# One core, a long convolution and a gated feed-forward block, forward and backward: exponent tables and d h kept on chip, two allocation stacks, and DMA transposes inside the forward DFTs

## Chip, cores and metric

The kernel runs on one core of one Trainium2 chip. The metric is the device time of one execution in microseconds (us); lower is better. The kernel before takes 1195.09 us (median of 4 runs, 1191.68 to 1198.79). Engines are named as in the profile: PE is TensorE, PEld its weight loads, DVE is VectorE, ACT is ScalarE, POOL is GpSimd, SP is SyncE; SPq is SP's instruction stream, which issues nearly all DMAs here. Each of these engines takes its own instructions in order. "d h" is the gradient at xn @ w1, "generation" the making of the convolution kernel K, and KF the tile that takes K out of PSUM.

## The reference, cut to what matters

L = 2048 positions, D = 512 channels, N = 128 states, F = 1792 hidden units, bf16 in and out. The kernel computes the output and the gradients of eleven inputs.

```python
xn = layernorm(x)
dt = exp(log_dt)[:, None]
P  = exp((dt * A)[:, :, None] * arange(L))            # 512 x 128 x 2048, complex: never built whole
K  = einsum("dn,dnl,dn->dl", C, P, dt * B).real       # the convolution kernel, one row per channel
y  = irfft(rfft(pad(xn)) * rfft(pad(K)))[:L] + xn * Dskip
g  = silu(silu(xn @ w1) @ w2)                         # the FFN gate
out = x + y * g
# and the vjp of all this for grad_out: d x, d A, d B, d C, d log_dt, d Dskip, d w1, d w2
```

## The kernel before

The program is a list of Python generators. Each `yield` ends a piece of work, and `interleave` deals the pieces of two generators alternately into the in-order instruction streams. The stages run in this order:

```python
    half = gen_half(k)                     # exponent tables of all four blocks -> DRAM (k.hd)
    ...
    interleave([half, gf], [1, 2])         # beside the FFN forward
    run(gf)
    ...                                    # pools closed, new pools opened
        run(gen_ssm_fwd(k, 0))             # convolution kernel ("generation") of block 0, alone
        for b in range(1, NB):
            interleave([gen_ssm_fwd(k, b), gen_conv(k, b - 1)], [1, 2])   # three mixed stages
        run(gen_conv(k, NB - 1))           # the last block's convolution, alone
        ...
        run(gen_dw2(k))                                        # weight gradient of w2
        interleave([gen_ffn_bwd(k), gen_ssm_bwd(k)], [1, 2])   # d h to DRAM, d x; gradients of the states
        run(gen_dw1(k))                                        # weight gradient of w1 (d h read back transposed)
        run(gen_ssm_final(k))                                  # parameter gradients, tail
```

A forward DFT (three per block, twelve in all) works in two steps with a transpose of 1 MB between them. TensorE does the transpose, and ACT evicts it (`ev` is `nc.scalar.copy` here):

```python
    B = big.tile([P, 2, G, P], BF16, name="dftB", tag="dftB")
    for g0 in range(0, G, 8):
        for c in range(2):
            pt = psumT.tile([P, 8, P], BF16, name="pt_b", tag="pt")
            for gi in range(8):
                nc.tensor.transpose(out=pt[:, gi, :], in_=A[:, c, g0 + gi, :, :]..., identity=k.ident[:])
            ev(B[:, c, g0:g0 + 8, :], pt[:])
        yield
```

The tables are made block by block. POOL copies parts of them (the last lines of `gen_half`), and the whole goes through DRAM:

```python
        for h in range(2):
            nc.gpsimd.tensor_copy(out=vXH[:, h, 0:2, :, :, 1], in_=vXH[:, h, 0:2, :, :, 0])
            nc.gpsimd.tensor_copy(out=vYL[:, h, :, :, 1]..., in_=vYL[:, h, :, :, 0]...)
            yh = T4[:, h, OYH:HSZ].rearrange("p (a u) -> p a u", u=2)
            nc.gpsimd.tensor_copy(out=yh[:, :, 1], in_=yh[:, :, 0])
            nc.gpsimd.tensor_scalar(out=T4[:, h, OXH + 2048:OYL], in0=T4[:, h, OXH + 1024:OXH + 2048], scalar1=-1.0, ...)
        nc.sync.dma_start(k.hd[:, 2 * b:2 * b + 2, :], T4[:])
```

At the end of each piece of generation, two ACT evictions take the kernel values out of PSUM. PSUM holds them as (q, j); SBUF wants (j, q) with 64 values of q in a row:

```python
            for e in range(2):
                es = slice(64 * e, 64 * e + 64)
                k.ev_k(KF[es, :, qb:qb + QCH].rearrange("p j q -> p q j"), ps[es, :, e, :])
```

## Time and profile before

The engine totals stand first in the profile's page: busy time, its share of the span of 1186.1 us, and the number of instructions.

```profile
PE 775.2 (65%) x6033; PEld 459.1 (39%) x6033; DVE 744.3 (63%) x1126; ACT 650.0 (55%) x1091; POOL 136.7 (12%) x96
...
```

No engine is near full over the whole, so the stages have to be read one by one. This is the view of windows of the kernel before: the stretch, its length, the busy time of each engine with the count of its instructions, then the granted clock of TensorE (PEclk, as a share of full speed), the busy share of the DMA engines, and GB/s.

```profile
core 0: us, PE busy (x) PEld busy (x) DVE busy (x) ACT busy (x) POOL busy (x), PEclk, DMA share, GB/s
...
30.00:308.00 278.00, 131.29 (x512) 50.77 (x511) 210.54 (x244) 160.50 (x319) 120.03 (x46) 0.73 0.40 145
308.00:385.00 77.00, 50.53 (x627) 43.42 (x628) 57.34 (x95) 47.52 (x61) 0.00 (x0) 0.72 0.65 217
385.00:488.00 103.00, 78.17 (x983) 62.91 (x983) 78.35 (x120) 93.93 (x146) 0.00 (x0) 0.88 0.41 122
...
695.00:763.00 68.00, 48.79 (x424) 34.02 (x421) 27.83 (x37) 52.54 (x93) 0.78 (x1) 0.87 0.19 47
763.00:859.00 96.00, 56.78 (x225) 22.89 (x226) 8.56 (x9) 4.09 (x7) 6.23 (x2) 0.82 0.96 220
859.00:1109.00 250.00, 195.75 (x960) 87.54 (x958) 162.60 (x271) 81.06 (x148) 0.00 (x0) 0.88 0.82 223
...
```

| stretch, us | what runs | what the line shows |
|---|---|---|
| 30 to 308 | FFN forward and tables | 278 us, and nothing is full: PE 131, DVE 211 of 278 us; POOL 120 |
| 308 to 385 | generation of block 0 alone | DVE 57 of 77 us |
| 385 to 695 | three mixed stages of about 103 us | ACT 94 of 103 us: the fullest engine |
| 695 to 763 | last convolution alone | ACT 53 of 68 us |
| 763 to 859 | w2 gradient | DMA share 0.96, PE 57 of 96 us |
| 859 to 1186 | backward, w1 gradient, tail | PE 196 of the first 250 us |

The change touches three pieces of work here (KF, the POOL copies, and the DFT transposes with their evictions to dftB); Vb stands beside them for comparison. A group's line reads: source line, engine, operation, output and input, shapes, count, then busy us and mean ns of one, then the idle time of the engine before them and what ended most of it.

```profile
L74 ACT CAST KF<-ps_k 64x256 bf16<-64x256 f32 x64 | 84.6, 1321 | 4.1 <-PE ps_k L564 3.6
...
L74 ACT CAST Vb<-psV 128x512 bf16<-128x512 f32 x128 | 67.5, 595 | 124.5 <-PE psV L737 84.9
...
L454 POOL COPY T_370<-T_370 128x1024 bf16<-128x1024 bf16 x8 | 62.7, 7841 | 82.2 <-DVE T_370 L60 82.2
...
L74 ACT COPY dftB<-pt_b 128x1024 bf16<-128x1024 bf16 x48 | 46.2, 1054 | 3.4 <-PE pt_b L95 3.3
L95 PE MATMUL pt_b<-ident_bfloat_80,dftA 128*128 128x128 bf16 x384 | 31.8, 236 | 17.9 <-ACT dftB L74 10.7 <-ACT dftA L74 4.7 <-ACT YTf L74 2.3
...
```

Two means are odd. The kernel eviction KF takes 1321 ns for 256 values per partition, while Vb, twice as wide, takes 595 ns on the same engine. And the POOL copy takes 7841 ns on average. The view of one tile, the table T, shows that this mean hides two kinds of copy (min/median/max in ns):

```profile
L454 POOL COPY T_370<-T_370 x8: 1032/1384/26786, 82.5 to 262.5; 128x1024 bf16<-128x1024 bf16 x8
```

The waits in the FFN stage (line that waited, what ended the wait, total us, times, longest) show PE waiting for the tanh evictions 76.8 us, and DVE waiting 38.2 us until a table had gone to DRAM:

```profile
PE ps_h L478 <- ACT th L482: 76.8, 10, 35.5
DVE T_370 L60 <- DMA hd<-T_370: 38.2, 2, 22.9
...
```

### The profile page before, as it was taken

What the parts mean: (1) busy time and instruction counts of PE and PEld (TensorE: products, weight loads), DVE (VectorE), ACT (ScalarE), POOL (GpSimd) and SP (SyncE); (2) the same over time, 40 slices, a digit from 0 to 9 for tenths busy, and PEclk for the clock granted to TensorE, in tenths of its full rate; (3) what the DMA queues carried; (4) which work ended last, traced back from release to release, by engine and by line L of the source; (5) the groups of instructions that cost most, each with busy time, mean ns of one, the idle gap of its engine ahead of it and who ended that gap; (6) DMA issues with size and microseconds to landing.
All of it is one profiled execution on the core that took longest, in us unless ns stands there. A gap on an engine that the chain in (4) does not pass through costs nothing. (4 is left out here: it accounts for less than half of the span.)

```text
span 1186.1 us, 15777 instructions
## 1 busy us (share of the span) xinstructions
PE 775.2 (65%) x6033; PEld 459.1 (39%) x6033; DVE 744.3 (63%) x1126; ACT 650.0 (55%) x1091; POOL 136.7 (12%) x96
## 2 busy tenths in 40 slices
PE   1462261367477777877777777546896886867693
PEld 1220020123266656656665654412342342423242
DVE  8788665896687759857965914600076575756153
ACT  4787362745177997999799797400042332323110
POOL 3229294360000000000000000200000000000000
PEclk9896675778777988899899888778998988988697
DMA  6221506538764513841651350499876889788981
GB/s 204 59 83 46 205 21 257 212 113 306 259 212 158 178 55 120 219 151 72 159 188 54 119 123 1 114 247 203 203 240 183 236 230 245 225 221 216 204 185 47
DMA packets 273262, 194.90 MB, mean 164 GB/s; under 512 B 189666, under 2 KB 250979, under 8 KB 271651
## 3 DMA queue, kind: packets, MB, share of 16 engines
q1 hardware_dynamic: 271842, 188.13, 55.0%
q0 software_dynamic: 768, 3.67, 0.9%
q10 hardware_dynamic: 576, 2.10, 0.6%
q8 instruction: 47, 0.77, 0.3%
q14 instruction: 29, 0.23, 0.1%
HBM read 84.28 MB, written 86.25 MB: 144 GB/s over the span
## 5 line engine op out<-in xcount | busy, mean ns | idle before, releaser
L74 ACT CAST Vb<-psV 128x512 bf16<-128x512 f32 x128 | 67.5, 595 | 124.5 <-PE psV L737 84.9
L478 PE MATMUL ps_h<-XNT,W_403 128*128 128x512 bf16 x224 | 67.0, 451 | 102.9 <-ACT th L482 76.8
L519 DVE TENSOR_TENSOR X<-H 128x1024 bf16<-128x1024 bf16 x128 | 83.8, 689 | 74.5 <-PE ps_k L564 64.6
L540 PE MATMUL pf_t<-ident_bfloat_80,X 128*128 128x128 bf16 x1024 | 93.8, 254 | 49.7 <-ACT KF L74 27.3
L540 PEld LDWEIGHTS <-X 128*128 128x128 bf16 x1024 | 80.3, 116 | 60.7 <-issue 52.6
L74 ACT CAST KF<-ps_k 64x256 bf16<-64x256 f32 x64 | 84.6, 1321 | 4.1 <-PE ps_k L564 3.6
L478 PEld LDWEIGHTS <-W_403 128*128 128x128 bf16 x224 | 23.7, 109 | 160.9 <-issue 144.4
L74 ACT CAST XTf<-pf_t 128x512 bf16<-128x512 f32 x128 | 67.4, 621 | 17.3 <-PE pf_t L540 17.1
L60 DVE TENSOR_TENSOR T_370<-MG,RC 128x896 bf16<-128x896 f32 (+1 forms) x32 | 49.2, 1615 | 43.0 <-DMA hd<-T_370 38.2
L737 PE MATMUL psV<-XT,Gbd 128*128 128x256 bf16 x256 | 48.1, 323 | 40.5 <-DMA XT<-xt_d 40.2
L454 POOL COPY T_370<-T_370 128x1024 bf16<-128x1024 bf16 x8 | 62.7, 7841 | 82.2 <-DVE T_370 L60 82.2
L713 POOL MEMSET Gbd<- 64x4096 bf16 x2 | 7.0, 3505 | 493.9 <-PE ps_i_7911 L130 493.9
L495 PE MATMUL ps_o<-W_405,aT 128*128 128x512 bf16 x224 | 57.2, 415 | 5.2 <-ACT th L482 5.2
L737 PEld LDWEIGHTS <-Gbd 128*128 128x128 bf16 x256 | 34.5, 178 | 64.9 <-DMA XT<-xt_d 30.4
L662 PE MATMUL ps_da<-DOT,W2T 128*128 128x512 bf16 x224 | 57.1, 400 | 0.2
L674 PE MATMUL ps_dx<-W1T,dhT 128*128 128x512 bf16 x224 | 56.3, 408 | 0.0
L632 PEld LDWEIGHTS <-A_ft 128*128 128x128 bf16 x224 | 22.7, 105 | 73.9 <-DMA A_ft<-at_d 28.7
L74 ACT COPY dftB<-pt_b 128x1024 bf16<-128x1024 bf16 x48 | 46.2, 1054 | 3.4 <-PE pt_b L95 3.3
L564 PE MATMUL ps_k<-YY,X 128*128 128x64 bf16 x1024 | 42.7, 203 | 7.1 <-ACT KF L74 6.6
L564 PEld LDWEIGHTS <-X 128*128 128x128 bf16 x1024 | 40.7, 105 | 9.8 <-issue 8.6
L95 PE MATMUL pt_b<-ident_bfloat_80,dftA 128*128 128x128 bf16 x384 | 31.8, 236 | 17.9 <-ACT dftB L74 10.7
L74 ACT COPY YTf<-pt_t 128x1024 bf16<-128x1024 bf16 x32 | 34.6, 1080 | 13.6 <-issue 8.5
(1576 smaller groups left out, 1932.3 us busy)
## 6 DMA issues: line engine op xcount, KB each, us to landing
hd<-T_370 SPq DMA_DIRECT2D x4, 4096.0 KB, 11.9
H<-hd SPq DMA_DIRECT2D x8, 2048.0 KB, 9.1
xt_d<-XTf SPq DMA_DIRECT2D x32, 512.0 KB, 3.1
XT<-xt_d SPq DMA_DIRECT2D x32, 512.0 KB, 4.5
YT<-yt_d SPq DMA_DIRECT2D x128, 128.0 KB, 4.5
yt_d<-YTf SPq DMA_DIRECT2D x32, 256.0 KB, 2.0
ut_d<-u SPq DMA_DIRECT2D x28, 256.0 KB, 2.4
at_d<-aT SPq DMA_DIRECT2D x4, 1792.0 KB, 6.8
```

The lines of the kernel that those rows point to most:

```text
L60: nc.vector.tensor_tensor(out=out, in0=a, in1=b, op=ALU.mult)
L74: self.nc.scalar.copy(out=out, in_=in_)
L95: nc.tensor.transpose(out=pt[:, gi, :], in_=A[:, c, g0 + gi, :, :].rearrange("p t e -> p (t e)"), identity=k.ident[:])
L454: nc.gpsimd.tensor_copy(out=vYL[:, h, :, :, 1].rearrange("p c g r l -> p c g (r l)"), in_=vYL[:, h, :, :, 0].rearrange("p c g r l -> p c g ...
L478: nc.tensor.matmul(out=ps[:], lhsT=W1[:, dk, ft * P:(ft + 1) * P], rhs=XNT[:, dk, 4 * tcn:4 * tcn + 4, :], start=(dk == 0), stop=(dk == DK ...
L495: nc.tensor.matmul(out=pso[:], lhsT=aT[:, ft, tt * P:(tt + 1) * P], rhs=W2[:, ft, :], start=(ft == 0), stop=(ft == FT - 1))
L519: nc.vector.tensor_tensor(out=out.rearrange("p (r h l u) -> p r h l u", h=nh, l=4, u=2), in0=h, in1=l, op=ALU.mult)
L540: nc.tensor.matmul(out=pf[:, qi, m // 2, :], lhsT=X[:, m, q + qi], rhs=k.ident[:], start=(m % 2 == 0), stop=(m % 2 == 1))
L564: nc.tensor.matmul(out=ps[:, q].rearrange("p e j -> p (e j)"), lhsT=X[:, m, q], rhs=YY[:, m // 2, q // 2, 1, 64 * (q % 2):64 * (q % 2) + 6 ...
L662: nc.tensor.matmul(out=ps[:], lhsT=W2T[:, dk, ft * P:(ft + 1) * P], rhs=DOT[:, dk, ls], start=(dk == 0), stop=(dk == DK - 1))
L674: nc.tensor.matmul(out=ps[:], lhsT=dhT[:, ft, tt * P:(tt + 1) * P], rhs=W1T[:, ft, :], start=(ft == 0), stop=(ft == FT - 1))
L737: nc.tensor.matmul(out=psV[:, qi].rearrange("p a b -> p (a b)"), lhsT=Gbd[:, :, :, :, 32 * (q_ // 2 % 2) + 4 * c + 2 * (q_ % 2) + q_ // 4] ...
```

## The change

Its intent: (1) compute the tables in eight halves just ahead of their use, keep them in SBUF, drop the DRAM round trip and POOL's copies; (2) split SBUF into a left and a right stack of pools, so that a stage can start before the pools of the other side close. This puts seven sixteenths of the generation beside the FFN, the generation of block b+1 beside the convolution of block b, and the last convolution beside the first backward work; (3) keep d h in SBUF, so that the w1 gradient uses TensorE transposes in place of a DRAM round trip; (4) let DMA transposes do the transposes inside the forward DFTs; (5) write KF in the other order.

The diff, cut to its core (cuts marked `...`):

```diff
@@ dft_fwd
     B = big.tile([P, 2, G, P], BF16, name="dftB", tag="dftB")
-    for g0 in range(0, G, 8):
-        for c in range(2):
-            pt = psumT.tile([P, 8, P], BF16, name="pt_b", tag="pt")
-            for gi in range(8):
-                nc.tensor.transpose(out=pt[:, gi, :], in_=A[:, c, g0 + gi, :, :]..., identity=k.ident[:])
-            ev(B[:, c, g0:g0 + 8, :], pt[:])
-        yield
+    for c in range(2):
+        nc.sync.dma_start_transpose(out=B[:, c], in_=A[:, c].rearrange("p g t e -> p (g t e)"))
+    yield
@@ main
+    def pool(name, side, bufs=1):
+        return tc.tile_pool(name=name, bufs=bufs, side=side, reuse_waits="tile")
 ...
-    interleave([half, gf], [1, 2])
 ...
-        run(gen_ssm_fwd(k, 0))
-        for b in range(1, NB):
-            interleave([gen_ssm_fwd(k, b), gen_conv(k, b - 1)], [1, 2])
-        run(gen_conv(k, NB - 1))
+        interleave([gen_ffn_fwd(k), BoundedGen(gs, 42)], [1, 1])     # gs: all of the generation
 ...
+    for b in range(NB - 1):
+        upto(b)
+        interleave([BoundedGen(gs, 26), gen_conv(k, b)], [1, 2])
 ...
+    interleave([gen_conv(k, NB - 1), BoundedGen(gb, 24)], [2, 1])    # gb: backward of blocks 0 to 2
 ...
+            interleave([chain([gd, gen_dh(k)]), gb], [2, 1])         # gd: w2 gradient; gen_dh: d h and w1 gradient
+        def final():
+            yield from gen_ssm_bwd(k, NB - 1)
+            for b0, nb in ((0, NB - 1), (NB - 1, 1)):                # the final step in two parts
+                with pool("fin", "left") as k.fin:
+                    yield from gen_ssm_final(k, b0, nb)
+        with pool("dxp", "right", 2) as k.dp:
+            interleave([gen_dx(k), final()], [1, 3])
@@ gen_ssm_fwd
-                k.ev_k(KF[es, :, qb:qb + QCH].rearrange("p j q -> p q j"), ps[es, :, e, :])
+                k.ev(KF[es, :, ql:ql + QCH], ps[es, :, e, :].rearrange("p q j -> p j q"))
@@ gen_half -> ssm_prep, half_angles, half_tables: the table k.T4 stays in SBUF
-            nc.gpsimd.tensor_copy(...)           # three copies and a scaling per half
-        nc.sync.dma_start(k.hd[:, 2 * b:2 * b + 2, :], T4[:])
+        nc.vector.tensor_copy(out=bl(1), in_=bl(0))   # one small copy left, the rest by broadcast
@@ gen_dh (from gen_ffn_bwd and gen_dw1): d h stays in k.dhT
-            nc.sync.dma_start_transpose(out=DH[:, j], in_=k.dht_d[(f0 + j) * P:(f0 + j + 1) * P, :])
+                nc.tensor.transpose(out=pt[:, j, :], in_=k.dhT[:, ft, (t0 + j) * P:(t0 + j + 1) * P], identity=k.ident[:])
@@ gen_ssm_final(k, b0, nb)
-        nc.sync.dma_start(k.outs[8].rearrange("(k p) -> p k", p=P), ddt_b[:])
+        nc.sync.dma_start(k.outs[8][bs].rearrange("(k p) -> p k", p=P), ddt_b[:])
```

## The prediction

> **What bounds the kernel now.** The kernel has four stages (first and last starts of each tile's instructions): the FFN forward with the exponent tables, 30 to 305 us; the kernel-generating stage of block 0 alone, 308 to 385; four convolution blocks, three beside the next generation, about 103 us each, the last alone, 68 us, to 763; backward to 1186. No engine bounds all: busy times are PE 775, DVE 744, ACT 650 us. By windows of 40 us: in the FFN stage DVE is busiest (31 to 37 us) and waits for POOL and the table write (one line idles 38 us until the table's DMA lands); in the convolutions ACT is busy 33 to 40 of 40 us; from 760 to 840 the DMA share is 0.97 while PE has 16 and 27 of 40 us (transposed loads: two 512 KB tiles, then both weights, hold the DMA queue); afterwards PE has 25 to 40 of 40 us; the chain of waits ends in a 26 us tail.
>
> **Removed.** The tables' DRAM round trip (33 MB) and POOL's table copies (115 us on POOL). 384 PE transposes (31.8 us) with 48 evictions to dftB (ACT 46.2 us). d h written to DRAM and loaded transposed (14.7 MB). The generation of block 0 alone, the last convolution alone and the separate last gradient stage disappear as stages of their own. The eviction of the kernel (1321 ns for 64x256, 64 times) gets another order; I take it as 30% cheaper.
>
> **Added.** 24 DMA transposes, on-chip to on-chip, of 512 KB. The trace has the same size from DRAM: 14 took a median 2.3 us on the queue and 4.8 us to landing, so I estimate 7 us for the pair of one DFT, against 2.7 us PE plus 4.2 us ACT removed: about 3 us more latency per DFT, twelve times, mostly hidden except in the last block. Table work goes to DVE in eight halves, by the times of the old operations about 17 us each, and 12 us each on ACT with table switches. 280 PE transposes of d h and of the gradient, at 83 ns busy each (as the removed ones) 25 us, and 29 us of evictions. A second read of the tanh, with 45 us of DVE work moved from forward to backward.
>
> **Sum.** Engine totals hardly change; the gain is overlap. Setup to about 42 us (7 us of parameter work goes first). FFN, generation and three convolutions: DVE about 475 us, ACT about 500; at the 88% that ACT reached in the old convolutions, 560 us, to 602 (before: 695). Last convolution beside the first backward generation: 85, to 687. Second and first weight gradient and d h with two backward blocks: PE 227 us at the old 80%, 284, to 971. d x with the last block: PE 79 us, 99, to 1070, and 8 us of tail. Prediction: 1080 us, 8 in 10 between 1010 and 1165. Faster by over 2%: 0.84; within: 0.10; slower: 0.06.
>
> **What would show it.** PE without a gap like 760 to 840; no hd in the DMA list; POOL near idle; the DFT stage waiting less than 10 us for dftB's DMA; convolutions with DVE and ACT both over 85% busy.
>
> **What would make it wrong.** The on-chip transposes. The Trainium skill, "DMA: Bandwidth & Descriptors", trn3 fast-DGE section, says that on earlier generations such a transpose is pushed tile by tile; no trace here has one with an on-chip source. If it holds the queue for 10 us instead of 2, every DFT waits and blocks the other DMAs behind it: 12 times 15 us would eat the whole gain. Second: in-order engines keep DVE waiting at the table hand-over, as the table has one buffer. Third: a lower granted clock with a busier PE.

## More of the kernel before

The tail writes d log_dt, 512 bf16 values held as 128 partitions x 4, so that neighbours in DRAM come from different partitions:

```python
    with nc.allow_non_contiguous_dma(reason="1 KB"):
        nc.sync.dma_start(k.outs[8].rearrange("(k p) -> p k", p=P), ddt_b[:])
```

## The result and the profile after

The changed kernel takes 1063.2 us (median of 4 runs, 1061.63 to 1068.18), and its outputs are correct. The ratio to the kernel before is 0.8903, with a 95% interval of 0.886 to 0.8946. A ratio is the mean time of one kernel's runs over the mean of the other's runs of the same rounds, so it is not quite the ratio of the medians. Where differences are given in us between two variants below, they are the difference of their ratios times 1191 us (the kernel before, run beside the experiments, had medians of 1190.4 to 1191.7), so that different chips do not enter. The 95% intervals of the ratios reach 3 to 6 us to either side, so a difference of a few us between two variants is not shown.

The engine totals of the kernel after (span 1059.9 us):

```profile
PE 719.4 (68%) x5834; PEld 424.4 (40%) x5897; DVE 734.9 (69%) x1196; ACT 576.5 (54%) x1014; POOL 20.7 (2%) x85
...
```

ACT lost 74 us of busy time and POOL 116, PE 56, DVE 9. Not all of PE's 56 us is work removed: the granted clock was 0.867 over this run and 0.835 before, and matmuls that both kernels have take less time each. The 1024 of pf_t are 93.8 us before and 78.0 after, the 256 of psV 48.1 and 42.8. What the clock itself is worth in the total was not separated. The windows of the kernel after:

```profile
core 0: us, PE busy (x) PEld busy (x) DVE busy (x) ACT busy (x) POOL busy (x), PEclk, DMA share, GB/s
0.00:60.00 60.00, 11.74 (x99) 10.00 (x101) 48.61 (x127) 27.05 (x28) 13.67 (x83) 0.83 0.40 105
60.00:245.00 185.00, 155.92 (x1392) 89.10 (x1412) 167.28 (x270) 156.11 (x278) 0.00 (x0) 0.94 0.57 182
...
368.00:485.00 117.00, 78.52 (x950) 61.22 (x951) 104.11 (x155) 89.68 (x163) 0.00 (x0) 0.81 0.53 124
...
660.00:743.00 83.00, 60.55 (x247) 25.52 (x254) 14.80 (x16) 8.20 (x15) 0.00 (x0) 0.84 0.99 219
743.00:885.00 142.00, 126.44 (x811) 65.74 (x824) 93.42 (x117) 49.08 (x70) 0.00 (x0) 1.00 0.56 161
...
1000.00:1060.00 60.00, 0.00 (x0) 0.00 (x0) 27.05 (x82) 3.25 (x6) 0.00 (x0) 0.52 0.12 26
...
```

Read it beside the table of before. The FFN with seven sixteenths of the generation now takes 185 us, with PE, DVE and ACT all between 84 and 90% busy; before, the FFN with the tables of all blocks took 278 us. The mixed stage has not become shorter (117 us against 103), though ACT is now only 90 of 117 us busy. It also makes tables now, which ran beside the FFN before, and DVE is busy 104 of 117 us where it was 78 of 103. The w2 gradient still has the DMA engines full (0.99) and takes 83 us. The d h stage is the best one (PE 126 of 142 us). And the last 60 us have no matmul at all, where before the last matmul ended 20 us before the end.

Two groups answer to those of before. The KF eviction costs 381 ns in place of 1321, and the weight loads of the second DFT step have idle time that ends when the transposed data lands:

```profile
L74 ACT CAST KF<-ps_k 64x256 bf16<-64x256 f32 x64 | 24.4, 381 | 7.8 <-PE ps_k L552 7.3
...
L98 PEld LDWEIGHTS <-C_267 128*128 128x128 bf16 x48 | 5.9, 122 | 57.7 <-DMA dftB<-dftA 51.5 <-issue 5.0 <-PE ps_k L552 0.6
```

The view of the tile dftB of the kernel after shows the DMA transposes (time in the SP stream, min/median/max ns), who waited (us, times), and the time from issue to landing:

```profile
L92 SPq DMA_TRANSPOSE dftB<-dftA x24: 1767/2477/4463, 260.0 to 627.5; - x24
...
  PEld L98: 51.5, 12
...
DMA to landing us min/median/max: 4.3/4.9/6.5
```

The wait comes twelve times, once per DFT, and lasts 1.6 to 9.1 us (4.3 in the mean). The chain that ended last, in order of time (start us, us, what), shows the new tail:

```profile
1014.57 14.32 DMA out_dram<-ddt_b_10283
1028.90 0.34 SPq L846
1029.30 0.41 SPq L846
...
1035.78 1.61 DMA S_10362<-s_d
...
```

One store of 384 bf16 values takes 14.3 us, and the loads at L846 of the second part of the final step (block 3 alone) wait for it. They have no data in common with the store, so the wait must come from SBUF space that is used again; this is read from the code and not tested. The waits of SP in the last 60 us (us, times, longest) show this store and the last one:

```profile
SPq L905 <- DMA out_dram<-ddt_b_10452: 16.1, 1, 16.1
SPq L846 <- DMA out_dram<-ddt_b_10283: 10.6, 1, 10.6
...
```

The DMA list of the last 60 us (issuer, count, size, median us to landing) adds that the loads which were issued just after that store took nearly as long as the store:

```profile
n_Ar_10290<-in_A_A_re_dram SPq DMA_DIRECT2D x1, 32.0 KB, 14.1
...
out_dram<-ddt_b_10283 SPq DMA_DIRECT2D x1, 0.8 KB, 14.3
...
```

The second such store, of 128 values, is the last thing in the program (L905).

### The profile page after: what moved, and what is told of

It reads as the page before. It is cut to its first block, busy times and chain, and to the rows that moved or that the text cites. A ratio compares the mean times of both kernels' runs of the same rounds, so it can differ in the third digit from the quotient of the medians.

```text
span 1059.9 us, 15298 instructions
## 1 busy us (share of the span) xinstructions
PE 719.4 (68%) x5834; PEld 424.4 (40%) x5897; DVE 734.9 (69%) x1196; ACT 576.5 (54%) x1014; POOL 20.7 (2%) x85
## 5 line engine op out<-in xcount | busy, mean ns | idle before, releaser
L502 DVE TENSOR_TENSOR X<-T_511 128x1024 bf16<-128x1024 bf16 x128 | 84.7, 706 | 33.8 <-PE ps_k L552 33.8
L528 PE MATMUL pf_t<-ident_bfloat_78,X 128*128 128x128 bf16 x1024 | 78.0, 235 | 30.3 <-DVE X L502 13.9
L586 PE MATMUL ps_h<-XNT,W_408 128*128 128x512 bf16 x210 | 53.0, 389 | 2.6 <-ACT th L590 1.5
L60 DVE TENSOR_TENSOR T_511<-PC 128x896 bf16<-128x896 f32 (+1 forms) x40 | 51.7, 1365 | 0.4 <-ACT PC L448 0.4
L781 PE MATMUL psV<-XT,Gbd 128*128 128x256 bf16 x256 | 42.8, 292 | 8.4 <-DMA XT<-xt_d 7.4
L74 ACT COPY DH<-pt_dh 128x1024 bf16<-128x1024 bf16 x28 | 27.9, 1035 | 36.2 <-PE pt_dh L708 36.1
L545 PE MATMUL pt_t<-ident_bfloat_78,YY 128*128 128x128 bf16 x256 | 27.4, 236 | 23.3 <-DVE YY L540 13.2
L702 DVE SCALAR_TENSOR_TENSOR dhT<-th_ft,ps_da 128x512 bf16<-128x512 bf16 x56 | 35.5, 681 | 8.3 <-PE ps_da L701 8.1
L589 ACT ACTIVATE aT<-ps_h 128x512 bf16<-128x512 f32 x56 | 37.4, 669 | 1.1 <-PE ps_h L586 0.6
L590 ACT ACTIVATE th<-ps_h 128x512 bf16<-128x512 f32 x56 | 37.8, 674 | 0.0
L600 PEld LDWEIGHTS <-aT 128*128 128x128 bf16 x224 | 22.1, 104 | 36.7 <-issue 18.9
```

Source lines behind the costliest of these rows:

```text
L60: nc.vector.tensor_tensor(out=out, in0=a, in1=b, op=ALU.mult)
L74: self.nc.scalar.copy(out=out, in_=in_)
L502: nc.vector.tensor_tensor(out=out.rearrange("p (r h l u) -> p r h l u", h=nh, l=4, u=2), in0=h, in1=l, op=ALU.mult)
L528: nc.tensor.matmul(out=pf[:, qi, m // 2, :], lhsT=X[:, m, q + qi], rhs=k.ident[:], start=(m % 2 == 0), stop=(m % 2 == 1))
L586: nc.tensor.matmul(out=ps[:], lhsT=W1[:, dk, ft * P:(ft + 1) * P], rhs=XNT[:, dk, 4 * tcn:4 * tcn + 4, :], start=(dk == 0), stop=(dk == DK ...
L589: nc.scalar.activation(out=aT[:, ft, :], in_=pf, func=ACT.Silu)
```

## The experiments

Twelve more kernels were run. All results are correct. "Old" kernels are edits of the kernel before, the others of the kernel after. Theory A says throughout that waits between in-order engines decide: a removed cost is worth what it frees in such a chain, and an added latency in a chain costs. The rival says what each quoted text says of it.

| run | kernel | us, median (range) | ratio to before | against its parent |
|---|---|---|---|---|
| after | the change | 1063.2 (1061.63 to 1068.18) | 0.8903 | |
| e1_pe_dft | after, PE transposes in the DFTs | 1023.54 (1020.88 to 1026.74) | 0.8596 | 37 us faster |
| e2_old_dma_dft | old, DMA transposes alone | 1215.74 (1210.27 to 1218.04) | 1.0203 | 24 us slower |
| e3_old_kf | old, KF order alone | 1138.33 (1137.09 to 1141.95) | 0.9556 | 53 us faster |
| e4_new_kf_old | after, old KF order | 1097.4 (1093.89 to 1102.81) | 0.9219 | 38 us slower |
| e5_row_store | after, d log_dt stored as rows | 1035.33 (1031.92 to 1038.71) | 0.8685 | 26 us faster |
| e6_prep_late | after, parameter work later | 1058.97 (1053.31 to 1062.65) | 0.8889 | within noise |
| e7_no_overlap | after, FFN and generation apart | 1084.97 (1080.92 to 1086.6) | 0.9106 | 24 us slower |
| e8_pe_dw2 | after, PE transposes in the w2 gradient | 1067.19 (1065.28 to 1071.71) | 0.8956 | not faster |
| e9_old_no_pool | old, table copies on DVE | 1147.22 (1145.9 to 1151.69) | 0.9626 | 45 us faster |
| e10_pair | after, two DFTs staggered | 1029.34 (1027.8 to 1031.25) | 0.863 | 33 us faster |
| e11_best | e1 and e5 together | 1007.96 (1004.7 to 1009.68) | 0.8447 | 54 us faster |
| e12_old_small | old, three local edits | 1084.05 (1081.84 to 1084.84) | 0.9085 | 109 us faster |

### The DFT transposes undone: e1_pe_dft

```diff
-    for c in range(2):
-        nc.sync.dma_start_transpose(out=B[:, c], in_=A[:, c]...)
-    yield
+    (the loop of the kernel before: 8 PE transposes into PSUM, one eviction, four times)
```

> The changed kernel with the forward DFTs' transposes back on TensorE (the DMA transposes undone, all else kept). Theory A (the gain is overlap; in the new convolution stage the in-order TensorE waits for the DMA transposes, 51 us of weight loads and some 20 us of matmuls waiting for dftB in the trace, while ScalarE has slack there): the waits for dftB go, ScalarE gets back about 46 us of evictions that it has room for, so faster than the changed kernel by 15 to 35 us, about 1030 to 1048 us. Theory B (the gain is ScalarE work removed from stages that ScalarE bounds): slower than the changed kernel by 20 to 45 us, about 1085 to 1105 us.

Measured: 1023.54 us, 37 us faster than the change, although 46 us of ACT evictions and 30 us of PE transposes came back. Theory A's direction held, and its 15 to 35 us were a little small. The part of the change that took work off two engines made the kernel slower: 37 us over twelve DFTs are 3 us each.

### The DFT transposes alone, in the old kernel: e2_old_dma_dft

The edit is the first hunk of the change, nothing else.

> The kernel before with only the forward DFTs' transposes moved to DMA. ScalarE is busy about 94 of 103 us in its convolution blocks, and 46 us of evictions go. Theory A: each DFT gets about 3 us more latency, part of the relief is lost to waiting, and the block that stands alone gets longer by about 10 us: between 20 us faster and 10 us slower. Theory B: ScalarE bounds the stage and the whole relief is gained, 35 to 46 us faster, about 1150 us.

Measured: 1215.74 us, 24 us slower than before. Both theories missed: A had allowed a loss of 10 us at most, the rival had expected a gain of most of the 46 us that ACT is relieved of. (The ratio's interval, 1.0168 to 1.0237, lies around 2% but clear of 1.) The view of the tile dftB in this run says why ACT's relief did not show:

```profile
L92 SPq DMA_TRANSPOSE dftB<-dftA x24: 1503/2293/6714, 392.1 to 755.2; - x24
...
  PEld L98: 53.0, 12
  PE ps_s L98: 50.6, 12
...
DMA to landing us min/median/max: 4.3/4.4/8.9
```

TensorE stands before the second step in each of the twelve DFTs, its weight loads 53.0 / 12 = 4.4 us and its matmuls 50.6 / 12 = 4.2 us in the mean (the two waits run side by side; single ones last 0.4 to 10.3 us). It takes its instructions in order, so the generation's matmuls that stand behind that step in the stream wait too. The three mixed stages became 115, 112 and 113 us long (103 before), with ACT 85 us busy in each. So ACT was the fullest engine of those stages, but not what 46 us of relief could turn into time.

### The latency hidden, the DMA transposes kept: e10_pair

If latency in the order of the stream is the cost, then work between the issue of a transpose and its use must win most of it back, with the same DMAs. The first steps of the U and the K transform now both come before the second steps; the K transform's intermediate tiles lie in two buffers that are free at that time.

```diff
-    yield from dft_fwd(k, k.xn[:, :, blk], UX, k.ev)
-    yield from dft_fwd(k, k.K_b[b][:], KX, k.ev, addc=...)
+    Bs = []
+    yield from dft_fwd1(k, k.xn[:, :, blk], k.ev, Bs)                       # step 1, issue the transposes
+    yield from dft_fwd1(k, k.K_b[b][:], k.ev, Bs, ("PX", "DX"))
+    yield from dft_fwd2(k, Bs[0], UX, k.ev)                                 # step 2
+    yield from dft_fwd2(k, Bs[1], KX, k.ev, addc=...)
```

> The changed kernel, DMA transposes kept, but the first steps of the first two forward DFTs of a block are run one after the other, with buffers that are idle then, before either second step: the transposes of eight of the twelve DFTs get matmuls of another DFT to hide behind. Theory A (the cost of the DMA transposes is their latency, 3 us net per DFT, met by an in-order TensorE): 10 to 25 us faster than the changed kernel, 1038 to 1053 us, not below the version with TensorE transposes (1024). Rival (the cost is the DMA queue and engines taken from other transfers): within 8 us of the changed kernel.

Measured: 1029.34 us, 33 us faster than the change and 4 us behind e1, which the intervals do not separate. The waits for dftB became fewer; the same view:

```profile
L99 SPq DMA_TRANSPOSE dftB<-dftA x24: 1721/2680/4650, 256.2 to 590.8; - x24
...
  PEld L110: 18.8, 5
  PE ps_s L110: 17.2, 5
...
```

Twelve waits of the weight loads with 51.5 us became five with 18.8. Told apart by transform: the eight that are staggered waited 35.5 us in the changed kernel and 1.3 us here (one of them); the four third transforms, which are not staggered, 16.1 and 17.5 us. The transposes themselves did not change: they take a median 2.7 us in the SP stream and 4.9 us to landing in this run. So the loss was latency in the stream, not the load on the DMA engines. The gain is above what theory A had expected (10 to 25 us), and about the fall of that one wait (33 us); the granted clock is nearly the same (0.870 against 0.867). The same staggering with TensorE transposes was not run, so what the new order would be worth without the latency is not known.

### The KF eviction, both ways: e3_old_kf and e4_new_kf_old

```diff
 # e3, in the kernel before
-                k.ev_k(KF[es, :, qb:qb + QCH].rearrange("p j q -> p q j"), ps[es, :, e, :])
+                k.ev_k(KF[es, :, qb:qb + QCH], ps[es, :, e, :].rearrange("p q j -> p j q"))
 # e4, in the kernel after: the same line back to the old order
```

> The kernel before with only the order of the KF evictions changed (the write runs along 8 neighbours instead of jumping 64 elements; in the changed kernel's trace one takes 381 ns instead of 1321). About 60 us of ScalarE work go, 15 us per block of 128 channels. Theory A: in the three mixed blocks ScalarE's relief is partly taken up by the next limit (DVE has 76 of 103 us, PE 78), so 25 to 40 us faster, about 1155 to 1170 us. Theory B: 45 to 60 us faster, about 1135 to 1150 us.

> The changed kernel with the old order of the KF evictions. ScalarE gets about 60 us back. Theory A: ScalarE has slack in the new stages (156 of 185 us in the FFN stage, 89 of 120 in the mixed blocks), so 10 to 25 us slower than the changed kernel, 1073 to 1088 us. Theory B: 45 to 60 us slower, about 1110 to 1123 us.

Measured: e3 is 53 us faster than before, e4 38 us slower than the change. The group in e3:

```profile
L74 ACT CAST KF<-ps_k 64x256 bf16<-64x256 f32 x64 | 24.8, 387 | 2.2 <-PE ps_k L564 1.8
```

In e4 it is back at 1298 ns. In each pair the operands are the same PSUM and SBUF bytes; only the order of the walk differs. The old order writes each next value 64 elements (128 bytes) on in SBUF (in e4, whose KF is half as wide, 32 elements) and reads runs of 32 values in PSUM; the new one writes eight neighbours (16 bytes) and jumps in PSUM. The Trainium skill, "SBUF — State Buffer", section "Door 1: The DMA port swizzle", says that SBUF has 16-byte lines and that each access that crosses to a new line pays a penalty. These runs agree in direction, and give the size for an ACT write: (1321 - 381) ns over 256 values is 3.7 ns per value. The jumping PSUM read cost nothing visible: in the kernel before, an ACT eviction of 256 values in a row on both sides (o10b) takes 372 ns, and the new KF eviction a median 367.

In the old kernel 53 of the 60 us that ACT saved became time (the rival's reading, ACT as the limit, had the size right); in the new one 38 of 60 did. In the new mixed stages DVE is the fuller engine (104 of 117 us), which fits that a part of what ACT gains is not on the path; this was not tested further.

This sits beside e2 in an instructive way: 46 us less ACT work by DMA transposes made the old kernel slower, 60 us less by another order made it 53 us faster. The second kind adds no latency.

### The table copies: e9_old_no_pool

```diff
-            nc.gpsimd.tensor_copy(...)   # three, and nc.gpsimd.tensor_scalar, all in gen_half
+            nc.vector.tensor_copy(...)   # the same four operations on DVE; the DRAM round trip stays
```

> The kernel before with only POOL's copies of the tables (and the negation) moved to DVE; the write to DRAM and the reading back stay. Two of those copies take 22 and 27 us in its trace, others of the same form 1.3 us. Theory A (slow POOL copies hold the table's write-out, DVE waits for it in order, and ScalarE and TensorE of the FFN behind it): DVE gets some 25 us of work, the stalls shrink, the FFN stage of 278 us falls to 210 to 245, so 35 to 70 us faster, 1120 to 1157 us. Rival (the one table buffer and its way through DRAM are the limit, whoever copies): less than 20 us faster.

Measured: 1147.22 us, 45 us faster than before, with the tables still going through DRAM. The gain lies in the FFN stage: its last product (ps_o) starts at 261.1 us in place of 302.5. No engine waits for the tables' way to DRAM any more (DVE waited 38.2 us for it before), so the rival, that this way is the limit whoever copies, is refuted. The wait of the FFN's matmuls for the tanh evictions from 30 to 270 us:

```profile
PE ps_h L478 <- ACT th L482: 48.8, 10, 11.6
...
```

It was 76.8 us before, with one wait of 35.5. The windows of the kernel before around two visits of POOL show what happened there (the columns as above):

```profile
82.50:104.70 22.20, 9.52 (x35) 3.67 (x34) 22.20 (x27) 18.73 (x47) 22.19 (x2) 0.77 0.11 41
104.70:118.00 13.30, 0.38 (x1) 0.10 (x1) 9.05 (x7) 6.46 (x4) 12.86 (x8) 0.54 0.00 0
141.50:168.30 26.80, 20.44 (x78) 7.96 (x77) 26.63 (x33) 22.65 (x48) 26.77 (x2) 0.87 0.09 30
168.30:180.00 11.70, 0.00 (x0) 0.00 (x0) 0.42 (x1) 1.99 (x2) 11.70 (x8) 0.60 0.00 0
```

In the first and third stretch DVE is busy nearly without a gap (27 and 33 instructions), and one copy of POOL, 1.0 us at its fastest and 1.4 in the median, takes the whole stretch (22.2 and 26.8 us; the second POOL instruction counted starts at its end). In the second and fourth, POOL's operations run one after another, DVE does 7 and 1 instructions, and PE does next to nothing for 13 and 12 us. In the second stretch a DVE operation that takes 0.75 us elsewhere took 1.76. The Trainium skill, "SBUF — State Buffer", section "Who interferes with whom", describes this: DVE and GpSimd share a port pair under an exclusive lock for a whole instruction, and a DVE instruction with two SBUF inputs contends with a GpSimd instruction that reads SBUF. The trace agrees in both directions, and it shows the copy held up not by one DVE instruction but by a whole row of them. That the lock is the cause, rather than the in-order wait of DVE for POOL's result, was not separated for each stall; taking the POOL work away removed both.

### The FFN and the generation apart: e7_no_overlap

```diff
-        interleave([gen_ffn_fwd(k), BoundedGen(gs, 42)], [1, 1])
+        run(gen_ffn_fwd(k))
+        run(BoundedGen(gs, 42))
```

> The changed kernel with the FFN forward run alone and the same 42 steps of generation after it instead of between its steps. Theory A (the overlap of the two is a main part of the gain): 60 to 80 us slower than the changed kernel, 1123 to 1143 us. Rival: generation alone is already quick with the cheap KF eviction (old stage of 77 us for two halves, less 15), so 30 us slower or less, up to 1093 us.

Measured: 24 us slower than the change; theory A had said 60 to 80, the rival was right. The windows:

```profile
60.00:170.00 110.00, 104.04 (x451) 43.52 (x459) 58.07 (x109) 82.14 (x152) 0.00 (x0) 0.99 0.62 207
170.00:285.00 115.00, 65.95 (x970) 58.54 (x969) 114.03 (x167) 80.84 (x134) 0.00 (x0) 0.73 0.47 122
```

Alone, the FFN is full on PE (104 of 110 us) and the same seven sixteenths of the generation are full on DVE (114 of 115 us). Together they take 185 us where one after the other takes 225, and of those 40 us about 24 remain at the end. The surprise is the first line: with no table work beside it the FFN takes 110 us, where FFN and tables together took 278 before. Even without overlap, FFN and seven sixteenths of the generation (56 of the 128 products X) with their tables take 225 us (60 to 285); before, FFN, all tables and about five sixteenths (40 of 128) took 355 (30 to 385). So most of what this stage gained is not overlap. How it divides between table work that now comes later, work moved to the backward pass, and stalls that are gone was not separated here; e9 puts 45 us on POOL's copies.

### The tail: e5_row_store

```diff
-        nc.sync.dma_start(k.outs[8][bs].rearrange("(k p) -> p k", p=P), ddt_b[:])
+    pt = k.psumT.tile([DK, P], BF16, name="pt_dt" + sfx, tag="pt")
+    nc.tensor.transpose(out=pt[:], in_=ddt_b[:], identity=k.ident[:])
+    ddt_r = fin.tile([DK, P], BF16, name="ddt_r" + sfx)
+    nc.vector.tensor_copy(out=ddt_r[:], in_=pt[:])
+    nc.sync.dma_start(k.outs[8][bs].rearrange("(k p) -> k p", p=P), ddt_r[:])
```

> The changed kernel with the gradient of log_dt turned on TensorE and stored as rows of 128 elements instead of one element per descriptor (both of its two stores). In the changed kernel's trace the first such store takes 14.3 us and the loads of the last block's final step wait for it, and the second takes 16.1 us at the very end. Theory A (these two stores are the tail): 20 to 28 us faster than the changed kernel, about 1035 to 1043 us. Rival: the stores only hide another wait (the last DVE work and the program's end), so at most 12 us faster, 1051 us or more.

Measured: 1035.33 us, 26 us faster; theory A was right. The same kind of load that took 14.1 us beside the old store, in the DMA list of this run's last stretch:

```profile
n_Ar<-in_A_A_re_dram SPq DMA_DIRECT2D x1, 32.0 KB, 1.6
```

So the store delayed not only who waited for it but the loads that were issued just after it. The Trainium skill, "DMA: Bandwidth & Descriptors", section "Rules for kernel authors", says that a strided or non-contiguous last dimension lowers to one descriptor per element. The trace agrees: the 512 elements of the kernel before are 512 packets of 2 bytes. The times, however, do not follow the number of elements: 512 elements landed in 16.0 us in the kernel before, 384 in 14.3 in the kernel after, and SP waited 16.1 for the 128. Nor is the time spent moving them. In the kernel before, the 512 packets all lie between 1169.6 and 1170.0 us, no packet of any queue moves after 1170.5, and the store lands at 1184.7. What the store waits for in these 14 us is not shown.

### A later parameter stage: e6_prep_late

```diff
-        ssm_prep(k)
         phase_setup(k)
         phase_ln(k)
+        ssm_prep(k)
```

> The changed kernel with the preparation of the parameters recorded after the layernorm instead of before the setup. The FFN's first matmul stood at 59.5 us in the changed kernel, at 30 in the one before. Theory A: the FFN begins at about 40 us and the time falls by 8 to 18 us, to 1045 to 1055 us. Rival: DVE bounds the FFN stage (167 of 185 us busy), the same DVE work only moves, so within 5 us of the changed kernel.

Measured: 1058.97 us, ratio 0.8889 against 0.8903: no difference that the intervals separate. The FFN's first matmul moved only from 59.5 to 53.8 us. The rival was right: the work only changed places. Why the setup takes 60 us where it took 30 stays open beyond this: the added parameter work is there, but its place is not the reason.

### The w2 gradient without DMA transposes: e8_pe_dw2

```diff
-        nc.sync.dma_start_transpose(out=A_ft[:], in_=k.at_d[ft * P:(ft + 1) * P, :])
+        nc.sync.dma_start(a_r[:]..., k.at_d[ft * P:(ft + 1) * P, :])
+        for t0 in range(0, T, 8):     # 8 PE transposes into PSUM, one eviction, twice
+            ...
```

> The changed kernel with the 14 transposed loads of the activations in the second weight gradient replaced by plain loads of the same size and 224 TensorE transposes with 28 ScalarE evictions. The DMA engines are 0.99 busy in that stage of 83 us, TensorE 61 of 83. Theory A (the transposed loads are what fills the DMA engines): the stage shrinks to about 65 us, 10 to 25 us faster, 1038 to 1053 us. Rival: the bytes are the same and bound it, so within 5 us.

Measured: 1067.19 us, not faster. The window of this stage:

```profile
660.00:740.00 80.00, 62.95 (x452) 35.78 (x461) 11.48 (x15) 32.30 (x41) 0.00 (x0) 0.94 0.67 201
```

The DMA share fell from 0.99 to 0.67, but the stage is still 80 us. In place of the DMA engines PE waits 10.3 us in 13 waits for the evictions of its own transposes, once per tile, and has more to do itself. The stage changed its limit and kept its length; a version that transposes one tile ahead was not tried. Both theories' reasons missed in part here.

### The two faults mended, and three small edits to the old kernel: e11_best and e12_old_small

e11_best is e1 and e5 together. e12_old_small is the kernel before with the KF order of e3, the DVE copies of e9 and the row store of e5.

> The changed kernel with TensorE transposes in the DFTs and the row store of the log_dt gradient, the two edits that gained alone (37 and 26 us by the ratios). They lie in different stages, so they should add: 992 to 1003 us. If the tail were hidden by something else once the middle is shorter, above 1010.

> The kernel before with three small edits and none of the redesign: the order of the KF evictions, the table copies on DVE instead of POOL, the row store of the log_dt gradient. Theory A (about half of the change's gain is such local cost, the rest is stages laid over each other and traffic removed): 53 us from KF, 35 to 70 from the copies, about 13 from the store, so 1055 to 1095 us; the redesign with its two faults mended (about 997) stays 60 to 95 us ahead. Rival (the redesign is worth little beyond them): 1040 us or less.

Measured: e11_best takes 1007.96 us, ratio 0.8447 (0.8411 to 0.8483), and is the best version. It gains 54 us of the 63 that its two parts have alone; theory A's sum was 5 us or more too good. What is left in its tail is the second part of the final step: its 23 loads stand behind the first part's last store in SP's stream, which waits 4.8 us for its data, and are issued one by one, some 0.47 us apart, from 983.5 to 994.3 us. SP waits for no landing there before the last one of the program (0.8 us). The 8 us that the sum lacks are no more than the intervals of the four ratios allow together (about 8 us), so a loss is not shown.

e12_old_small takes 1084.05 us. Three edits of a few lines give 109 us, as theory A had said (1055 to 1095 us; the KF order and the copies gained 53 and 45 us alone, and it put the store at 13). The whole change is 22 us ahead of them; with its two faults mended it is 76 us ahead.

## Why the prediction was right or wrong

The time was right: 1080 predicted, 1063 measured, well inside 1010 to 1165. The sum got there with errors of opposite sign, so the closeness is partly luck. The table gives the prediction's own stages and the measured ones.

| stage | predicted us | measured us |
|---|---|---|
| setup | 42 | 60 |
| FFN, generation, three convolutions | 560 | 507 (60 to 567) |
| last convolution and first backward | 85 | 93 |
| w2 and w1 gradients, d h | 284 | 256 (660 to 916) |
| d x and the last block | 99 | 84 |
| tail | 8 | 60 |

- **"Engine totals hardly change; the gain is overlap."** Wrong. ACT fell by 74 us, PE by 56 (in part by the clock), POOL by 116. Pulling the overlap of FFN and generation apart costs 24 us (e7), while the KF order alone is worth 38 us in the new kernel (e4) and taking the copies off POOL 45 us in the old one (e9). What the overlap of the other stages is worth was not measured alone.
- **"I take it as 30% cheaper" (the KF eviction).** The mechanism was right, the size was off: 71% cheaper, 1321 to 381 ns. This is 35 us of ACT work more than the sum had (84.6 x 0.7 = 59.2 predicted, 24.4 measured), all of it in the stretch where "ACT about 500" became 386 us and "DVE about 475" 420 (60 to 567). Another 20 us or so are the tables: the sum had 8 times 12 us on ACT, their instructions take 77 us there. The rest of those 114 us was not traced. The guess had no measurement behind it, though the trace held one: Vb evicts twice the width in 595 ns.
- **"About 3 us more latency per DFT, twelve times, mostly hidden except in the last block."** The 3 us were right in size: e1 gives 37 us over 12, a net of waits and of the work that comes back, and the median transpose took 2.5 us in the queue and 4.9 us to landing against 2.3 and 4.8 estimated. "Mostly hidden" was the step that failed: the second step stood close behind in PE's stream, and the wait appears twelve times out of twelve, in every block. The prediction's own test was less than 10 us of waiting for dftB's DMA; the trace has 51.5.
- **The feared tile-by-tile push.** The prediction cited the Trainium skill, "DMA: Bandwidth & Descriptors", for it; the table of the section "Why a DMA increments its semaphore by 16 and not by 1" has the on-chip transpose of earlier generations at one push per tile. In these runs an on-chip source holds the queue for a median 2.48 us, much as one from DRAM (2.3 us), so the case of 10 us did not occur. The loss that came instead was smaller than the 12 x 15 us feared, and had another form. The fear of a lower granted clock did not come true either: 0.867 against 0.835.
- **"PE without a gap like 760 to 840."** Did not come: the w2 gradient still has a DMA share of 0.99, and PE 61 of 83 us. The change did not take its 14 transposed loads away, and e8 shows that taking them away moves the limit to PE and its evictions.
- **"No hd in the DMA list; POOL near idle."** Right: POOL 20.7 us, the table no longer goes to DRAM. In size the removal was undervalued: the table copies were costed as POOL time, but their harm was to DVE and PE (45 us in e9, with the DRAM round trip still in place).
- **"8 us of tail."** With the first long stage the largest error. The old tail of 26 us was read, but the 16.0 us that its last store took were not seen as such, and the change has that store twice, the first time in the middle of a dependency through reused space. e5 puts 26 us on it; the rest of the 60 us is mainly 14.6 us of DVE work of d x and of the first part, then the loads and the DVE work of the second.
- **"PE 227 us at the old 80%" and "PE 79 us, 99".** Both a little high: the weight gradients with d h have PE 210 of 256 us (82%), d x with the last block 73 of 84 (87%).
- **"Convolutions with DVE and ACT both over 85% busy."** Half right: DVE 104 of 117 us (89%), ACT 90 of 117 (77%).

What stays open: what d h on chip and the removal of the tables' DRAM trip are worth alone, how far the 76 us between e11 and e12 come from which overlap, what the higher granted clock is worth, and what the small stores wait for.

## What to carry to other kernels

Ask of a moved operation not only which engine it frees but what stands right behind it in an in-order stream: a DMA in place of two busy engines cost 37 us here, and issuing it one transform earlier gave 33 of them back. Compare each instruction's mean time with that of a neighbour of like size before a redesign: one eviction at 1321 ns, copies at 7841 ns and a 1 KB store of 16 us were worth 109 us in a few lines. When a sum of stages comes out right, check each stage, since here minus 53 and plus 52 us met.

## What the Trainium skill lacked or had wrong

- "SBUF — State Buffer", "Door 1: The DMA port swizzle": it names a penalty for crossing 16-byte lines, but no size for an ACT write. For an ACT eviction of 256 values the runs show 1321 ns with a 128-byte step of the write, 1298 with 64 bytes, and 381 ns with runs of 16 bytes. The page speaks of slow matmuls for non-contiguous PSUM; an ACT read that jumps in PSUM showed no cost (median 367 ns against 372 in a row).
- "DMA: Bandwidth & Descriptors", "Rules for kernel authors": one descriptor per element, but no time. A store of 128, 384 or 512 bf16 elements across partitions took 16.1, 14.3 and 16.0 us, not in proportion to the elements (the packets of the last lay within 0.4 us), and loads of 32 KB issued just after the one of 384 took 12.5 to 14.1 us where they take 1.6 to 2.4 us without it (e5).
- "DMA: Bandwidth & Descriptors", "DMA Transpose (X-bar)": no latency. A 512 KB on-chip transpose took 2.5 us in the issuing queue and 4.9 us to landing (medians of 24), and a kernel that used the result at once lost 3 us per transform against PE transposes.
- "SBUF — State Buffer", "Who interferes with whom": it has the rule, and a GpSimd slowdown of 1.5 times in passing, but not what a long row of DVE instructions does. Here a POOL copy of 1.4 us in the median took 22.2 and 26.8 us beside 27 and 33 of them.
